# w1's last 96 columns as extra columns of wqkv's third block, with all operations in a fixed order

## The chip, the cores and the metric

The kernel runs on one NeuronCore of a Trainium2 chip. The metric is device time in microseconds; an execution before the change takes 414.9 us (median of three runs, 414.75 to 414.92). One execution was recorded by the hardware profiler. Its page and the answers to queries on its trace are what the sections below quote.

## The reference

Two branches over the normalised input are multiplied and added to the input. Branch A is a causal, dilated sliding-window attention (window 8, step 2, 32 heads of 16), branch B a two-layer MLP on a second LayerNorm of the same rows.

```python
def _A_ref(x, wqkv, wo):                      # S=2048, D=512, H=32, W=8, dil=2
    qkv = (x @ wqkv).reshape(B, S, 3, H, Dh)  # then split and transposed
    ...
    logits = einsum("bhsd,bhswd->bhsw", q, kg) * Dh ** -0.5
    attn = softmax(where(mask, logits, -1e9))
    o = einsum("bhsw,bhswd->bhsd", attn, vg)
    return o.reshape(B, S, D) @ wo

def _B_ref(x, w1, b1, w2, b2):                # w1: 512x1376, w2: 1376x512
    y = _layernorm(x)
    h = gelu(y @ w1 + b1)
    return h @ w2 + b2

xn = _layernorm(x)
return x + _A_ref(xn, wqkv, wo) * silu(_B_ref(xn, w1, b1, w2, b2))
```

## The kernel before

**Tiling.** The 2048 positions fall into two interleaved halves (DIL = 2, since the attention steps by 2) of eight tiles with 128 positions each. Every fp32 operand is held as a high and a low fp16 part. A product is three fp16 matmul series: high by high, low by high and high by low. The normalised, transposed activations are in four buffers yT0 to yT3, one for each *chunk* of 512 positions (chunks 0 and 1 are the first half, 2 and 3 the second).

**Attention units.** There are eight units: two halves times four blocks (hb) of 128 columns of wqkv for each of q, k and v. For a unit, `qkv` (from L720) multiplies, tile by tile, a tile of yT as the stationary operand by 384 columns of weights in 12 matmuls (L746) into a PSUM buffer, and ACT (L763) or, in the first two units, sometimes VectorE (L759) scales it into the buffer U0 or U1, units taking turns. The DMA queue then copies shifted rows inside U (halos). `attention` (from L785) works on VectorE: four products q times k over 2048 columns (L805), each with a sum over the head (L808), a softmax with ACT's exponential (L831), and four products with v (L863; L901 in the last unit). POOL adds the first pair of those four (L873, 2048 columns), VectorE the second (L858), POOL does later folds (L883). The result is split into high and low parts (L846 on ACT, L848 on VectorE) and brought into the transposed buffer oT by a DMA transpose (L851).

**MLP.** w1's 1376 columns are eleven blocks f = 0 to 10, ten of 128 columns and a last one of 96. `mlp1` (L1016) uses a block of w1 as the stationary operand and streams a chunk's 512 positions past it, 12 matmuls for each chunk and block, also for the block of 96. ACT applies bias and GELU (L1033) and makes the high part of h (L1036), VectorE the low part (L1038). `mlp2` (L1052) adds h times w2 into four PSUM banks z0 to z3, one for each tile of the chunk: three matmuls for each bank and block. For the last block h lies in the buffer hlast with a row of ones under it, so that b2 is the 97th row of w2. Behind a chunk's last block ACT applies SiLU, and the gate goes to DRAM (gd). `wo_first` (L929) and `wo_last` (L961) multiply oT by wo and combine it with gate and input (L920, L943; L993, L997, L1000).

**The order.** All operations are entered into a plan with their readers, writers and estimated durations. `Plan.issue` places them one after the other: of the operations that are ready, on all engines, it takes one that can start earliest, a hand-set priority deciding among near ones, and so it fixes each engine's order of instructions. Each engine then runs its own list in that order, held back only by waits on what an instruction reads or overwrites. All DMAs are issued from the SP queue. Weight preparation (sums of squares over each weight for its scale, L421 and L514, then high and low parts, L482, L536, L486, L543) belongs to the first hundred microseconds. Some 24 small matmuls on a constant (L1169) run in the first microseconds of TensorE.

## Time and profile before

| | |
|---|---|
| median of three runs | 414.9 us |
| the profiled execution's own time | 415.18 us |
| its span, from the first to the last instruction | 413.4 us |
| mean granted TensorE clock | 0.999 |
| time between span and the execution's time | 1.8 us |

The page gives in part 1 each engine's busy time, its share of the span and its number of instructions; in part 2 the span in forty slices, one digit for a slice in tenths; in part 4 the chain that ended last. A group's line has its source line, engine, operation, output and input with their shape, the count, and then busy time, mean ns of one, idle time ahead of it and what ended that. A line of the timeline has start, length and work, and in brackets how long the engine was idle before and who ended it. DMA issue lines end in the median time from issue to landing.

### The profile page before, as it was taken

Reading aid. Unit: us, or ns where it says so; the run is one execution under the profiler, and the core shown is the slowest. Engines: PE = TensorE matmul, PEld = TensorE weight load, DVE = VectorE, ACT = ScalarE, POOL = GpSimd, SP = SyncE. Lnnn points to the kernel's source line nnn. Section 1 sums busy time; section 2 is a strip of 40 time slices with the busy share of each in tenths; the row PEclk is TensorE's granted clock in tenths of the full one; section 3 lists DMA queues with packets and bytes.
Section 4 is the critical chain, followed back from the end, with each engine's and each line's share of the span. In section 5 each row is a group of like instructions: output and inputs, shape, how many; then the busy total and the mean of one; then the engine's idle time right before and its main releaser. Section 6 shows DMA issues by size and latency. Waiting matters only on the chain.

```text
span 413.4 us, 5554 instructions
## 1 busy us (share of the span) xinstructions
PE 405.9 (98%) x2083; PEld 206.6 (50%) x2083; DVE 379.5 (92%) x379; ACT 222.1 (54%) x353; POOL 120.3 (29%) x131
## 2 busy tenths in 40 slices
PE   8799999999999999999999999999999999999996
PEld 5555544445654455445544554455455544444443
DVE  4996989998999999989998999999999998999954
ACT  4699899994549655843384252225212393263500
POOL 3834002004380425042504330434033404520021
PEclk9999999999999999999999999999999999999999
DMA  8958717030045137720172034223604244007133
GB/s 281 397 112 258 235 61 230 0 128 1 1 142 152 28 93 183 149 46 2 48 221 75 0 102 116 68 86 88 205 7 122 88 111 145 0 18 238 23 102 131
DMA packets 47211, 46.41 MB, mean 112 GB/s; under 512 B 31785, under 2 KB 32225, under 8 KB 46673
## 3 DMA queue, kind: packets, MB, share of 16 engines
q1 hardware_dynamic: 47184, 46.06, 37.6%
q8 instruction: 16, 0.26, 0.3%
q14 instruction: 11, 0.08, 0.1%
HBM read 24.06 MB, written 7.34 MB: 76 GB/s over the span
## 4 chain that ended last, share of the span: by engine, by line
PE 92%; ACT 3%; issue 1%; DVE 1%; POOL 1%; ACTq 0%
PE z L1052 28%; PE ps L1016 28%; PE ps L746 25%; PE ps L929 5%; PE ps L961 2%; PE z L961 2%; PE pl L746 1%; ACT w L421 1%; PE pl L961 1%; ACT f L673 1%; ACT yT L687 0%; ACT wq L536 0%; POOL wq L471 0%; POOL rb L635 0%; ACT prod L661 0%
## 5 line engine op out<-in xcount | busy, mean ns | idle before, releaser
L1016 PE MATMUL ps<-yT,w 128*128 128x512 f16 (+1 forms) x528 | 120.4, 379 | 0.0
L746 PE MATMUL ps<-wq,yT 128*128 128x384 f16 x708 | 117.0, 326 | 0.2 <-DVE U L759 0.2
L1052 PE MATMUL z<-w,h 128*128 128x512 f16 x480 | 110.4, 379 | 0.0
L746 PEld LDWEIGHTS <-yT 128*128 128x128 f16 x744 | 72.5, 98 | 49.2 <-issue 1.0
L1016 PEld LDWEIGHTS <-w 128*128 128x128 f16 (+1 forms) x528 | 52.8, 100 | 61.0
L805 DVE TENSOR_TENSOR prod<-U 128x2048 f32<-128x2048 f32 x32 | 73.2, 2286 | 2.2 <-POOL prod L883 0.7
L1052 PEld LDWEIGHTS <-h 128*128 128x128 f16 x480 | 46.6, 98 | 55.5 <-issue 0.3
L808 DVE TENSOR_REDUCE L<-prod 128x128 f32<-128x2048 f32 x32 | 73.0, 2281 | 0.4
L1033 ACT ACTIVATE ps<-ps,b1T,hsc 128x512 f32<-128x512 f32 (+1 forms) x44 | 32.9, 748 | 73.4 <-PE ps L1016 72.2
L863 DVE TENSOR_TENSOR prod<-pl,U 128x2048 f32<-128x2048 f32 x28 | 63.2, 2283 | 4.2 <-POOL prod L873 4.1
L763 ACT ACTIVATE U<-ps,cs 128x384 f32<-128x384 f32 x54 | 31.2, 580 | 65.2 <-PE ps L746 65.2
L873 POOL TENSOR_TENSOR prod<-prod,prod 128x2048 f32<-128x2048 f32 x7 | 31.7, 4531 | 113.8 <-DVE prod L863 99.6
L883 POOL TENSOR_TENSOR prod<-prod 128x1024 f32<-128x1024 f32 x14 | 32.9, 2349 | 0.0
L882 POOL COPY gate<-prod 1x1 f32<-1x1 f32 x21 | 5.5, 264 | 91.0 <-DVE prod L805 82.2
L1038 DVE SCALAR_TENSOR_TENSOR h<-ps,hsc,h 128x512 f16<-128x512 f32 x40 | 29.6, 741 | 1.7 <-ACT h L1036 1.4
L1036 ACT ACTIVATE h<-ps,hsc 128x512 f16<-128x512 f32 x40 | 27.3, 684 | 1.3 <-PE z L1052 0.4
L929 PE MATMUL ps<-wo,oT 128*128 128x512 f16 x96 | 21.7, 379 | 0.0
L858 DVE TENSOR_TENSOR prod<-prod,prod 128x2048 f32<-128x2048 f32 x9 | 20.5, 2282 | 0.0
L1033 ACT ACT_TABLE_LOAD x10 | 12.8, 1283 | 8.6 <-PE ps L1016 8.5
L883 POOL TENSOR_TENSOR prod<-prod,prod 128x1024 f32<-128x1024 f32 x7 | 16.4, 2347 | 0.0
L961 PEld LDWEIGHTS <-oT 128*128 128x128 f16 x108 | 10.6, 98 | 10.4
L929 PEld LDWEIGHTS <-oT 128*128 128x128 f16 x96 | 9.4, 98 | 11.2
(179 smaller groups left out, 377.8 us busy)
## 6 DMA issues: line engine op xcount, KB each, us to landing
f<-in_A_x_dram SPq DMA_DIRECT2D x31, 256.0 KB, 3.5
U<-U SPq DMA_DIRECT2D x16, 392.0 KB, 4.0
gd<-f SPq DMA_DIRECT2D x12, 256.0 KB, 3.4
prod<-in_A_x_dram SPq DMA_DIRECT2D x8, 256.0 KB, 6.9
oT<-in_B_w_dram SPq DMA_DIRECT2D x2, 1024.0 KB
yT<-in_B_w_dram SPq DMA_DIRECT2D x2, 1024.0 KB, 7.9
f<-gd SPq DMA_DIRECT2D x8, 256.0 KB, 2.7
out_dram<-f SPq DMA_DIRECT2D x8, 256.0 KB, 2.8
```

The lines of the kernel that those rows point to most:

```text
L746: nc.tensor.matmul(b.t[:, 0:384], y[:, s, k, o:o + P], wq[:, hb, t, k], start=(n == 0), stop=(n == 11))
L763: act(384, lambda i=i, b=b: nc.scalar.activation(U3[:, i:i + 31:15, :], b.t[:, 0:384].rearrange("p (t e) -> p t e", t=3), AF.Identity, sca ...
L805: dve(2048, lambda p2=p2, g=g: nc.vector.tensor_tensor(p2(), q, slots(Ut, KH, 2 * g), op=ALU.mult), qk + [("kh", ub, 0), ("kh", ub, 1), (" ...
L808: dve(2048, lambda pr=pr, g=g: nc.vector.tensor_reduce(L3()[:, 2 * g:2 * g + 2], pr.t.rearrange("p (r f d) -> p r f d", r=2, d=DH), AX.X, ...
L863: dve(2048, lambda: nc.vector.tensor_tensor(pr.t.rearrange("p (r f d) -> p r f d", r=2, d=DH), A3()[:, 2 * g:2 * g + 2].rearrange("p r (f ...
L873: pool(4.75, lambda: nc.gpsimd.tensor_tensor(acc.t, acc.t, p1.t, op=ALU.add), [acc, p1], [acc])
L883: nc.gpsimd.tensor_tensor(x.t[:, 0:1024], x.t[:, 0:1024], y(), op=ALU.add)
L929: nc.tensor.matmul(b.t, oT[:, hb, i // 4, s, i % 4], wo[:, t, hb], start=(hb == 0 and n == 0), stop=(hb == last and n == 2))
L961: nc.tensor.matmul(b.t[:, cols], oT[:, hb, i // 4, s, i % 4], wo[:, t, hb, cols], start=(start and hb == 0 and n == 0), stop=(stop and hb ...
L1016: nc.tensor.matmul(b.t[0:M], w1[:, s, f * 512 + k * M:f * 512 + (k + 1) * M], yT[ch][:, t, k], start=(n == 0), stop=(n == 11))
L1033: act(512, lambda: nc.scalar.activation(b.t[0:M], b.t[0:M], AF.Gelu_apprx_tanh, bias=b1T[0:M, f:f + 1], scale=hsc[0:M, 1:2]), [b, ("b1T",) ...
L1052: nc.tensor.matmul(z.t, hl[s][0:K, t * P:(t + 1) * P], w2[0:K, w, f], start=(f == 0 and n == 0), stop=(f == NF - 1 and n == 2))
```

## The change

Three things change together.

1. w1's last 96 columns move into the weight buffer of wqkv's third block (HLAST = 2), which becomes 480 columns wide. The 12 matmuls for each tile of the two units of that block (unit 2 and unit 6) now give q, k and v and, in columns 384 to 479, the last block's pre-activation with *positions on partitions* and features along the row. ACT takes these 96 columns out (L870 of the changed kernel) into an fp32 buffer for each chunk of the half (hl0 or the tile `first`). For each chunk the new function `last_block` fills the pad and the row of ones (POOL), adds the bias along the row (POOL), applies GELU (ACT), makes the high (ACT) and low part (VectorE), and lets a DMA transpose bring it to features on partitions, back into the same buffer. `mlp1` is no longer called for the last block, and `mlp2` takes its operand from there.
2. The order of all operations is a table of numbers, ORDER, that `issue` follows; the greedy choice is left for when the table is empty.
3. Some estimated durations of the plan, and which tile holds the identity and the constant 1/512, change.

```diff
+HLAST = 2
+ORDER = (
+    0, 1, 2, 19, 126, 110, 131, 118, 127, 108, 109, 122, 130, 120, 123, 237, 20, 21, 124, 111, 125, 22, 23, 117,
...
+)
...
-        order = []
+        order, fixed = [], [self.ops[n] for n in reversed(ORDER)]
         while len(order) < len(self.ops):
             best = None
-            for e, cand in engs.items():
+            if fixed:
+                o = fixed.pop()
+                t = max([self.earliest(o)] + [min(b.ring.free) for b in o.bufs if b.slot is None])
+                assert not o.npred and t < float("inf")
+                best = (t, o)
+            for e, cand in engs.items() if best is None else ():
...
-    wq = sb.tile([P, NHB, 2, KT, 384], F16, name="wq")
-    w1 = sb.tile([P, 2, KT * F], F16, name="w1")
+    wq = [sb.tile([P, 2, KT, 384 + FL * (hb == HLAST)], F16, name=f"wq{hb}") for hb in range(NHB)]
+    w1 = sb.tile([P, 2, W1C[3]], F16, name="w1")
+    wl = wq[HLAST][:, :, :, 384:384 + FL]
...
+    def last_block(ch):
+        n = 4 * FL
+        h16 = R_f.new()
+        v = lambda: h16.t.bitcast(F16).rearrange("p (a t f) -> p a t f", a=2, t=4)
...
+        def pads():
+            nc.gpsimd.memset(v()[:, :, :, FL:P], 0.0)
+            nc.gpsimd.tensor_scalar(v()[:, 0, :, FL], halves[:, 8:12], hsc[:, 2:3], 2.0, op0=ALU.mult, op1=ALU.mult)
+        with prio(PEV):
+            pool(0.9, pads, [("hsc2",), ("hp", j, 0), ("hp", j, 1)], [(h16, 2)], port=False)
+            pool(1.0, lambda: nc.gpsimd.tensor_tensor(x3(), x3(), row, op=ALU.add), xk + [("b1T",)], xk)
+            act(n, lambda: nc.scalar.activation(x, x, AF.Gelu_apprx_tanh), xk, xk,
+                aps=1, table="gelu")
+            act(n, lambda: nc.scalar.activation(v()[:, 0, :, 0:FL], x3(), AF.Identity, scale=hsc[:, 2:3]),
+                xk + [("hsc2",)], [(h16, 0)])
+            dve(n, lambda: nc.vector.scalar_tensor_tensor(v()[:, 1, :, 0:FL], x3(), hsc[:, 2:3], v()[:, 0, :, 0:FL],
+                                                          op0=ALU.mult, op1=ALU.subtract),
+                xk + [(h16, 0)], [(h16, 1)], c=0.125)
+            dst = hlt[ch % 2].rearrange("p a (t x) -> p (a t) x", t=4)
+            dma(P * 2048, lambda: nc.sync.dma_start_transpose(dst, h16.t.bitcast(F16)), [(h16, k) for k in range(3)],
+                [("hl", ch % 2)], rate=140e3, issue=1.3, tail=1.2)
...
-                    nc.tensor.matmul(b.t[:, 0:384], y[:, s, k, o:o + P], wq[:, hb, t, k],
+                    nc.tensor.matmul(b.t[:, 0:wide], y[:, s, k, o:o + P], wq[hb][:, t, k],
                                      start=(n == 0), stop=(n == 11))
...
+            if hb == HLAST:
+                act(FL, lambda i=i, b=b: nc.scalar.activation(
+                    hpt[i // 4][:, (i % 4) * FL:(i % 4 + 1) * FL], b.t[:, 384:384 + FL], AF.Identity, scale=hsc[:, 1:2]),
+                    [b, ("hsc",)], [("hp", i // 4, i % 4)], prio=PEV, after=pl.users([("hp", i // 4, i % 4), ("hl", i // 4)]))
+        for j in range(2 if hb == HLAST else 0):
+            last_block(2 * c + j)
...
     def mlp2(ch, f):
-        hi, lo, K, h, hk = hq.pop(f)
+        if f < NF - 1:
+            hi, lo, K, h, hk = hq.pop(f)
+        else:
+            hi, lo, K = (lambda: hlt[ch % 2][:, 0]), (lambda: hlt[ch % 2][:, 1]), FL + 1
+            h = hk = ("hl", ch % 2)
...
-            if p < len(steps):
+            if p < len(steps) and steps[p][1] < NF - 1:
```

Where the order differs, three places. In the rows below a line number, the operation, output and inputs with their buffer numbers, and the shape; L-numbers of the changed kernel differ from those before.

**ACT, from the start of the kernel.** prod0 and U1 hold wqkv's first and second block as loaded, oT, o160 and h0 parts of w1 as loaded; squares are L514 and L421 before, L588 and L495 now. Before:

```order
L514 ACT_TABLE_LOAD
L514 ACTIVATE wq_78,s1_122<-prod0_93 128x768 x2
L536 ACTIVATE wq_78<-prod0_93,qsc_148 128x384 x4
L514 ACTIVATE wq_78,s3_124<-U1_87 128x768
L687 CAST yT0_82<-z30_146 128x4x128
L514 ACTIVATE wq_78,s3_124<-U1_87 128x768
L659 ACTIVATE rb0_151<-pb0_150,rb0_151 128x1
L661 ACTIVATE prod2_95<-prod2_95,rb0_151 128x512
```

Now:

```order
L588 ACT_TABLE_LOAD
L588 ACTIVATE wq0_77,s1_124<-prod0_95 128x768
L588 ACTIVATE wq1_78,s2_125<-U1_89 128x768
L588 ACTIVATE wq0_77,s1_124<-prod0_95 128x768
L610 ACTIVATE wq0_77<-prod0_95,qsc_150 128x384 x3
L588 ACTIVATE wq1_78,s2_125<-U1_89 128x768
L610 ACTIVATE wq0_77<-prod0_95,qsc_150 128x384
L733 ACTIVATE rb0_153<-pb0_152,rb0_153 128x1
L735 ACTIVATE prod1_96<-prod1_96,rb0_153 128x512
L761 CAST yT0_84<-z30_148 128x4x128
L495 ACTIVATE w1_81,s5_128<-o160_107 128x1024
```

A square over the second block now stands between the two squares over the first, and the first square over w1 comes earlier. 76 matmuls of 384 columns before, and 60 now, stand on TensorE ahead of the matmul that totals w1's squares (L435, now L509).

**VectorE, the end of attention 0.** The four products with v read U0 (L863 before, L972 now). Before:

```order
L863 TENSOR_TENSOR prod2_95<-pl0_142,U0_86 128x2048
L863 TENSOR_TENSOR prod1_94<-pl0_142,U0_86 128x2048
L863 TENSOR_TENSOR prod0_93<-pl0_142,U0_86 128x2048
L1038 SCALAR_TENSOR_TENSOR h1_107<-ps2_141,hsc_154,h1_107 128x512
```

Now:

```order
L972 TENSOR_TENSOR prod2_97<-pl0_144,U0_88 128x2048
L972 TENSOR_TENSOR prod1_96<-pl0_144,U0_88 128x2048
L972 TENSOR_TENSOR prod0_95<-pl0_144,U0_88 128x2048
L1143 SCALAR_TENSOR_TENSOR h2_110<-ps2_143,hsc_156,h2_110 128x512
L617 SCALAR_TENSOR_TENSOR wq2_79<-yT2_86,qsc_150,wq2_79 128x2x384 x2
L972 TENSOR_TENSOR prod1_96<-pl0_144,U0_88 128x2048
```

Two low parts of wqkv's third block now stand ahead of the fourth product. Ahead of that product stand, over all, two low parts of h and one of hlast, two single ones of w2 and two of wqkv fewer than before.

**ACT, the third block's first tiles (unit 2).** Before, the evictions of the unit come behind the GELU and the high part of hlast:

```order
L1036 ACTIVATE hlast_91<-ps1_140,hsc_154 96x512
L701 ACTIVATE mv1_159<-mv1_159 128x1
L703 ACTIVATE f2_98,mv1_159<-f2_98,mv1_159 128x512
L1033 ACTIVATE ps2_141<-ps2_141,b1T_90,hsc_154 128x512
L1036 ACTIVATE h2_108<-ps2_141,hsc_154 128x512
L763 ACTIVATE U0_86<-ps1_140,cs2_115 128x3x128
L482 ACTIVATE wo_81<-yT2_84,osc_158 128x1024
```

Now each tile has two evictions, and other work stands between the tiles:

```order
L870 ACTIVATE hl0_93<-ps2_143,hsc_156 128x96
L866 ACTIVATE U0_88<-ps2_143,cs2_117 128x3x128
L1141 ACTIVATE h1_109<-ps1_142,hsc_156 128x512
L870 ACTIVATE hl0_93<-ps0_141,hsc_156 128x96
L495 ACTIVATE wo_83,s6_129<-yT2_86 128x1024 x2
L866 ACTIVATE U0_88<-ps2_143,cs2_117 128x3x128
L773 ACTIVATE f4_102,mv1_161<-f4_102 128x512
L866 ACTIVATE U0_88<-ps0_141,cs2_117 128x3x128
```

The last block no longer passes through `mlp1` there. On TensorE the order of the matmul groups is finer than before: the three matmuls of one z bank now often stand alone between groups of 12. Ahead of unit 2's first matmul stand 168 matmuls of 384 columns in both orders, and of 512 columns 255 before and 213 now.

72 lines of the change are left out of this document (37 added, 35 removed), and 60 rows, old and new, of the table ORDER.

## The prediction

> **What bounds the kernel now.** I read the page's shares first, then the chain of waits in order of time, then the windows, then the groups kept apart by shape. Page, parts 1 and 2:
>
> ```profile
> span 413.4 us, 5554 instructions
> PE 405.9 (98%) x2083; PEld 206.6 (50%) x2083; DVE 379.5 (92%) x379; ACT 222.1 (54%) x353; POOL 120.3 (29%) x131
> ACT  4699899994549655843384252225212393263500
> PEclk9999999999999999999999999999999999999999
> ```
>
> A busy PE need not be a PE without gaps, so the chain decides (start, length, work), with the windows beside it (stretch, its length, then busy time of PE, PEld, DVE, ACT, POOL):
>
> ```profile
> 31.22 0.16 PE z L435
> 31.39 0.67 PE pl L746 x4
> ...
> 101.60 15.60 PE ps L746 x96
> ...
> 378.65 2.59 PE ps L1016 x12
> ...
> 408.45 1.32 PE ps L961 x12
> ...
> 409.80 0.49 DVE U L993
> ...
> 410.32 0.42 DVE U L1000
> 31.20:409.80 378.60, 378.50 (x1937) 189.91 (x1936) 353.82 (x309) 200.30 (x314) 104.05 (x107) 1.00 0.35 100
> 44.00:393.80 349.80, 335.62 (x277) 1.00 0.33 93
> ```
>
> From 31.2 to 409.8 TensorE has no gap worth a tenth of a microsecond. Three things therefore make the span: the head up to 31.2, in which ACT is the dense engine (digits 9 and 8), the matmul work, and 3.6 us of tail. VectorE is second: between its first attention product and its last head output (44.0 to 393.8, second window, DVE alone) it idles 14.2 of 349.8 us. A change can gain from the matmul work, the head or the tail, and lose by making TensorE wait.
>
> Rates come from the chain, where consecutive starts are real. Twelve 512-column matmuls take 2.59, so 216 ns each; 96 of 384 columns take 15.60, so 162.5 ns. The means in the group table (379 and 326) overlap and are not used.
>
> **The change part by part: TensorE.** w1's last block goes as matmuls of its own and comes back as 96 more columns on matmuls that run anyway.
>
> ```profile
> L1016 PE MATMUL ps<-yT,w 128*96 128x512 f16 x48 | 11.0, 379 | 0.0
> L746 PE MATMUL ps<-wq,yT 128*128 128x384 f16 x708 | 117.0, 326 | 0.2 <-DVE U L759 0.2
> ```
>
> Removed: 48 x 216 ns = 10.4 us. The old block used 96 of 128 output rows but paid for the full stream of 512 tokens. Widened: 16 token tiles x 12 = 192 matmuls. No row has 480 columns; between the two rates a column costs (216 - 162.5)/128 = 0.418 ns, so 96 cost 40 ns and 192 cost 7.7 us. Bounds: 0 if 480 went like 384, 10.3 (192 x 53.5) if like 512. I take 7.7, since the two rates are nearly proportional to columns. Net **-2.7 us**, between -10.4 and -0.1. The Trainium skill (TensorE: Matmul & The Clock Gate, "Wait — 56ns, not 53.3ns?") states N/2.4 GHz plus about 2.5 ns; both rows agree with it, and it would give 202.5 ns at 480 columns and the same -2.7. The second product (w2 with 97 rows) stays at 48 matmuls.
>
> **ACT, DVE, POOL, queue.**
>
> ```profile
> L763 ACT ACTIVATE U<-ps,cs 128x384 f32<-128x384 f32 x54 | 31.2, 580 | 65.2 <-PE ps L746 65.2
> L1036 ACT ACTIVATE h<-ps,hsc 128x512 f16<-128x512 f32 x40 | 27.3, 684 | 1.3 <-PE z L1052 0.4
> L1033 ACT ACTIVATE ps<-ps,b1T,hsc 96x512 f32<-96x512 f32 x4 | 3.0, 743 | 17.2 <-PE ps L1016 17.2
> L1033 ACT ACT_TABLE_LOAD x10 | 12.8, 1283 | 8.6 <-PE ps L1016 8.5
> L1038 DVE SCALAR_TENSOR_TENSOR h<-ps,hsc,h 128x512 f16<-128x512 f32 x40 | 29.6, 741 | 1.7 <-ACT h L1036 1.4
> L486 DVE SCALAR_TENSOR_TENSOR w<-h,hsc,w 128x384 f16<-128x384 f32 x1 | 0.6, 608 | 0.0
> L471 POOL TENSOR_TENSOR wq<-prod,wq 128x384 f16<-128x384 f32 x2 | 1.9, 928 | 0.2
> yT<-f SPq DMA_TRANSPOSE x12, 3.3
> ```
>
> ACT: 16 evictions of 96 columns at about 0.35 (580 less 288 columns at the 0.81 ns between the first two rows) are 5.6; four GELUs and four scalings of 384 columns at about 0.6 are 4.8; three more table loads are 3.8; removed are four GELUs and four scalings, 5.7. About +8.5 on an engine with some 190 us idle. Bounds for a small eviction: 0 and 0.58; even 9 us in all would be covered. DVE: 4 x 0.61 for 4 x 0.74, -0.5. POOL: four bias adds of 384 columns at 0.93 and four fills, bounded by 0 and the same 0.93, against removed fills of hlast; at most +7.5 on 120. Four DMA transposes with 3.3 us from issue to landing. All that late work has to be done before the w2 product of the last block: in the changed order 19 us of matmuls lie between the last widened tile of chunk 0 (tiles 0 to 3) and that product, while eviction, add, GELU, scaling, low part and landing come to 0.35 + 0.93 + 0.6 + 0.6 + 0.6 + 3.3 = 6.4. Hidden; were the cover gone, 6.4 per chunk would show.
>
> **The head.** What counts is when matmuls flow without gaps and how many are done by then. Before: 76 matmuls of 384 columns stand ahead of the total over w1 (L435), which starts at 31.22: as if the stream had begun at 31.2 - 76 x 0.1625 = 18.9. In the changed order 60 stand ahead of it, and ACT reaches it earlier, but its second operation is now a square over wqkv's second block.
>
> ```profile
> 4.49 0.84 ACT L514 ACTIVATE wq<-prod 128x768 bf16<-128x768 f32 x1 [2.48 <-DMA prod<-in_A_wqkv_dram]
> 6.84 0.84 ACT L514 ACTIVATE wq<-prod 128x768 bf16<-128x768 f32 x1 [1.41 <-DMA prod<-in_A_wqkv_dram]
> 8.92 2.13 ACT L536 ACTIVATE wq<-prod,qsc 128x384 f16<-128x384 f32 x4 [1.15 <-DVE qsc L459]
> 9.13 0.33 SPq L1126 DMA_DIRECT2D o<-in_B_w_dram  x1
> SPq L1126 <- DMA U<-in_A_wqkv_dram: 0.6, 1, 0.6
> 22.02 1.90 ACT L421 ACTIVATE w<-oT 128x2048 bf16<-128x2048 f32 x1
> ```
>
> The queue's issue at 9.13 waited for that block, so it lands at about 9.1. The two squares (0.95 each with their accumulator) then end at 11.0, and the first scaling starts after the same 1.15 of totals, near 12.1 instead of 8.92: 3.2 later. Behind it the work up to the last square of w1 is 16.6 us in the changed order (four scalings 2.1, one square 0.9, two scalings of 768 1.8, the w1 squares 5.9, three casts 1.6, two normalisations 2.0, two casts 1.2, two evictions 1.1): 28.7, the total at 28.9. Equivalent start: 28.9 - 60 x 0.1625 = 19.1, so +0.3 with no wait counted. The ACT waits of before in this stretch, 1.4 and 1.15 above among them, show what such a sum leaves open: I take **0**, bounds -1.5 and +1.5.
>
> **The tail.** The last product before is a 256-column piece; now it is three 512-column matmuls into z2, with a 512-column scaling and sum behind.
>
> ```profile
> L993 DVE SCALAR_TENSOR_TENSOR U<-z,osc,U 128x512 f32<-128x512 f32 x3 | 2.3, 750 | 3.0 <-PE z L961 3.0
> L1000 DVE TENSOR_TENSOR U<-U,f 128x512 f32<-128x512 f32 x4 | 3.3, 845 | 0.1
> out_dram<-U SPq DMA_DIRECT2D x7, 256.0 KB, 2.0
> out_dram<-U SPq DMA_DIRECT2D x2, 128.0 KB, 1.7
> ```
>
> 0.75 for 0.49, 0.69 (the sum at 0.845 in the mean, 0.69 where nothing disturbs it) for 0.42, 2.0 for 1.7: **+0.8**, bounds 0 and 1.0.
>
> **The waits that the new order could add.** The decisive place is the third block's first group. Matmul work ahead of it falls from 82.4 to 73.3 us (168 x 0.1625, and 255 or 213 x 0.216), so TensorE is there at 92.5 instead of 101.6. It has three ps banks; its third tile, at 92.5 + 2 x 2.43 = 97.4, needs the first one evicted into U0, and that needs attention 0 to have read U0.
>
> ```profile
> 98.47 2.28 DVE L863 TENSOR_TENSOR prod<-pl,U 128x2048 f32<-128x2048 f32 x1
> L543 DVE SCALAR_TENSOR_TENSOR wq<-yT,qsc,wq 128x768 f16<-128x768 f32 x4 | 3.8, 986 | 0.0
> 136.74 4.55 POOL L873 TENSOR_TENSOR prod<-prod,prod 128x2048 f32<-128x2048 f32 x1 [14.00 <-DVE prod L863]
> 140.32 1.52 DVE L713 TENSOR_TENSOR f<-f,f 128x512 f16<-128x512 f32 x1
> L713 DVE TENSOR_TENSOR f<-f,f x8: 675/680/1520, 140.3 to 177.6; 128x512 f16<-128x512 f32 x8
> ```
>
> Attention 0 now ends with three low parts of h and hlast (2.2), two of w2 (1.5) and two of wqkv (2.0) fewer ahead of it: 100.75 - 5.7 = 95.0. But one low part of wqkv comes 2.9 us behind the product that starts POOL's 4.55 us sum, and reads two SBUF tensors. The last two rows show what happens then: a 0.68 us sum stretched to 1.52, ending at 141.8 just after POOL's end at 141.3. So +1.6: 96.7, eviction 0.58, bank free at 97.3 against a need at 97.4. **0**, with no margin: every microsecond more on DVE costs TensorE one. The bounds are 0 and 14.2 (the idle that DVE now shows between 44.0 and 393.8, come once more on top). At the end DVE has slack:
>
> ```profile
> 392.97 0.75 DVE L848 SCALAR_TENSOR_TENSOR o<-prod,osc,o 128x512 f16<-128x512 f32 x1 [0.79 <-ACT o L846]
> oT<-o SPq DMA_TRANSPOSE x9, 4.4
> ```
>
> That last half of attention 7 ends at 393.7 and lands 4.4 later. In the changed order 5.5 us of matmuls stand from the first that needs it to the end (one tile of 256 columns whole, one of 512 whole, the late thirds of three), so for an end at 409.8 - 2.7 = 407.1 it may come as late as 397.2: 3.5 us of slack.
>
> **Sum.** -2.7 + 0 + 0.8 + 0 = -1.9 on the profiled execution's own time of 415.18 (span 413.4 and 1.8 around it): 413.3. The median of the runs shown is 414.9, 0.3 lower: **413.0 us**.
>
> **Rivals.**
> - **VectorE falls behind (slower).** Place: the pair sums on POOL (4.55 each, seven of them), behind which the new order puts more DVE operations with two SBUF operands; in the second unit a low part of wo follows only 1.3 us into the sum and could wait 3.3. Should the seven units lose 1.2 each on average, 8 us in all, the margins (0.1 here, about 4 at the end) leave TensorE waiting some 4 us: 417. It decides once DVE is 2 us later than the sum above has it. For it: the stretched row, and seven places. Against it: DVE's 14.2 us of idle, part of which can move. The Trainium skill (GPSIMD Engine Reference, "1. Specifications") states that POOL's SBUF interfaces are shared with VectorE, with contention for DVE instructions of two SBUF inputs; by that rule each such place costs, and the stretched row agrees. Chance 0.27.
> - **The head gains.** If ACT's early waits close up, 1.5 comes off the head, and 411.5 results. For it: fewer ACT operations ahead of the w1 total. Against: the late square. Chance 0.18.
> - **No net change.** The wide matmuls cost what 512 columns cost, -0.1, and the tail its 0.8: 415.6. Against it: the proportional rates. Chance 0.15.
> - **The forecast** keeps 0.40.
>
> **How the numbers follow.** A measurement here tells changes of about 0.2% (0.8 us). Faster: forecast and head, 0.58; within 0.2%: 0.15; slower: 0.27. The forecast's own range is 411.8 to 414.0. The range, with a tenth out on each side, takes in the head's gain with a little less stall or cheaper columns below (409.8), and the VectorE case above (418).
>
> **What would show it.** Right: 192 matmuls of 480 columns at 12 in 2.43 us; TensorE without gaps from near 29 to about 407; attention 0 read out near 96.7. Wrong: idle on PE ahead of the widened tiles released by ACT's evictions, DVE operations of 0.7 us stretched beyond 1.5 behind POOL's sums, a stream that starts to flow later than 31, or twelve wide matmuls in 2.59.

## The result, and the profile after

The changed kernel is slower: 429.1 us in the median (four runs, 427.2 to 430.9) against 414.9 for the kernel before (414.75 to 415.6). The ratio is 1.034, with a 95% interval of 1.029 to 1.039. The forecast was 413.0, with 409.8 to 418.0 as the range. The profiled execution is the fastest of the four, 427.23 us, with a span of 425.5 against 413.4; 12.1 us have to be found.

Page, parts 1, 2 and 4, of the changed kernel:

```profile
span 425.5 us, 5482 instructions
PE 404.8 (95%) x2035; PEld 200.6 (47%) x2035; DVE 393.7 (93%) x379; ACT 226.5 (53%) x372; POOL 128.7 (30%) x140
PEclk9999999999999999999999999999999999999996
PE 70%; DVE 16%; issue 5%; DMA 3%; ACT 2%; SPq 1%; DVEq 0%; ACTq 0%
```

VectorE has the same 379 instructions and is busy 14.2 us longer than before (393.7 against 379.5). It now holds 16% of the chain that ended last. The granted clock is whole until the last slice, in which TensorE is done.

The windows of the changed kernel (stretch, its length, then busy time of PE, PEld, DVE, ACT, POOL, the granted clock, the DMA share and GB/s) put TensorE's idle time in its places:

```profile
38.60:138.10 99.50, 94.58 (x464) 44.53 (x461) 94.85 (x100) 76.81 (x145) 32.21 (x32) 1.00 0.33 100
138.10:337.40 199.30, 199.30 (x1010) 98.81 (x1010) 191.66 (x140) 93.15 (x143) 64.75 (x71) 1.00 0.38 93
337.40:380.40 43.00, 41.96 (x209) 20.12 (x206) 42.41 (x27) 17.47 (x24) 12.70 (x13) 1.00 0.34 91
415.90:425.50 9.60, 0.61 (x3) 0.10 (x1) 2.61 (x3) 0.00 (x0) 1.27 (x1) 0.66 0.52 191
```

From 138.1 to 337.4 there is no gap at all. Before it 4.9 us are idle, after it 1.0. The last row begins with the first of the last two evictions and still has 0.6 us of matmuls in it, so from the end of the matmuls to the end of the span it is 9.0 us (9.60 - 0.61), where it was 3.6 before. What those gaps wait for is in the view of waits (engine, line, releaser, us in total, times, longest), of which these are the main rows behind the head:

```profile
PE ps L1125 <- DVE h L1143: 2.3, 2, 1.3
PE ps L1125 <- DVE s L522: 1.7, 1, 1.7
PE ps L1125 <- ACT first L870: 0.9, 1, 0.9
PE ps L1125 <- ACT U L866: 0.8, 1, 0.8
```

Busy ends are modelled, so a wait is sized better from start to start. The next fence shows how: six matmuls start at 135.35 and need 6 x 0.216 = 1.30, so the next was due at 136.65; it started at 138.10, 1.45 late, where the row says 1.29. Counted so, the gaps are 0.95 and 0.39 (at 51.6 and 55.0), 1.89 (110.5), 1.06 (123.7), 1.45 (136.4), 1.14 (362.9) and 0.25 (380): 7.1 us; each is named by the start of the last matmul ahead of it. A further 0.15 lies at 121.3. The kernel before has 0.2 behind its head (at 130.2).

**The stretched operations.** The timeline around one of these waits, that at 136.4 (start, length, engine, line, work, count, idle before) shows POOL's pair sum, VectorE behind it and TensorE behind VectorE:

```profile
132.32 4.52 POOL L982 TENSOR_TENSOR prod<-prod,prod 128x2048 f32<-128x2048 f32 x1 [4.80 <-PE z L1161]
132.87 4.52 DVE L787 TENSOR_TENSOR f<-f,f 128x512 f16<-128x512 f32 x1 [0.69 <-ACT f L786]
137.31 0.74 DVE L1143 SCALAR_TENSOR_TENSOR h<-ps,hsc,h 128x512 f16<-128x512 f32 x1
135.35 1.46 PE L1161 MATMUL z<-w,hl 97*128 97x512 f16 x6
138.10 2.75 PE L1125 MATMUL ps<-yT,w 128*128 128x512 f16 x12 [1.29 <-DVE h L1143]
```

The subtraction, 0.68 us where nothing disturbs it, starts 0.55 into the pair sum and ends 0.5 behind it. The low part of h stands behind it on VectorE, and only that low part frees the bank of ps that TensorE wants next. The largest stretch is beside the last of the seven pair sums:

```profile
346.15 4.82 POOL L982 TENSOR_TENSOR prod<-prod,prod 128x2048 f32<-128x2048 f32 x1 [11.44 <-DVE prod L972]
346.52 5.54 DVE L957 SCALAR_TENSOR_TENSOR o<-prod,osc,o 128x1024 f16<-128x1024 f32 x1
351.98 4.47 DVE L972 TENSOR_TENSOR prod<-pl,U 128x2048 f32<-128x2048 f32 x2
```

1.28 became 5.54, and the products with v behind it need the buffer that it reads. Against the plain time of its group, the operations stretched by over 0.25 us lose: 0.7 (L560 at 40.5), 1.3 and 1.7 (L617 at 90.3 and 102.2), 3.8 (L787), 1.1 (L815 at 182), 4.3 (L957), 0.5 (L1109 in the tail): 13.4 us against 2.6 before.

**The wait at 123.7 has another cause.** ACT's own order stands behind it:

```profile
121.47 1.28 ACT L940 ACT_TABLE_LOAD   x1
122.76 0.63 ACT L940 ACTIVATE L<-L 128x512 f32<-128x512 f32 x1
124.13 0.58 ACT L866 ACTIVATE U<-ps,cs 128x384 f32<-128x384 f32 x1 [0.73 <-PE ps L848]
124.61 0.56 ACT L870 ACTIVATE first<-ps,hsc 128x96 f32<-128x96 f32 x2
```

The eviction at 124.13 and the first of the two at 124.61 are of the unit's last tile, whose matmuls end at 124.1, and it is the bank of that tile that TensorE takes at 124.99. The tile ahead of it was done at 120.86, but its evictions (at 124.83 and 125.25) stand on ACT behind the exponential with its table load and behind those of the last tile. The exponential itself waited for nothing: what it reads was ready at 120.2.

**The tail.** The last matmuls, SP's queue, and the last work of POOL and VectorE:

```profile
413.11 3.40 PE L1070 MATMUL z<-wo,oT 128*128 128x512 f16 x15
413.86 8.63 SPq L1111 DMA_DIRECT2D out_dram<-U  x9
415.90 1.41 DVE L1102 SCALAR_TENSOR_TENSOR U<-z,osc,U 128x512 f32<-128x512 f32 x2 [0.84 <-PE z L1070]
416.73 1.27 POOL L1106 TENSOR_TENSOR U<-U,f 128x512 f32<-128x512 f32 x1 [2.90 <-DVE U L1102]
417.34 1.20 DVE L1109 TENSOR_TENSOR U<-U,f 128x512 f32<-128x512 f32 x1
```

All nine writes of the output are issued only from 413.86 to 422.49. The first waits for POOL's sum that ends at 413.83. The second is the write of the tile whose sum runs on POOL from 416.73 to 418.00. Seven writes stand behind it, six of them with sums that had ended by 415.1.

### The profile page after: what moved, and what is told of

Its sections match the earlier page's. It is cut to its first block, busy times and chain, and to the rows that moved or that the text cites. A ratio compares the mean times of both kernels' runs of the same rounds, so it can differ in the third digit from the quotient of the medians.

```text
span 425.5 us, 5482 instructions
## 1 busy us (share of the span) xinstructions
PE 404.8 (95%) x2035; PEld 200.6 (47%) x2035; DVE 393.7 (93%) x379; ACT 226.5 (53%) x372; POOL 128.7 (30%) x140
## 4 chain that ended last, share of the span: by engine, by line
PE 70%; DVE 16%; issue 5%; DMA 3%; ACT 2%; SPq 1%; DVEq 0%; ACTq 0%
PE ps L848 21%; PE z L1161 20%; PE ps L1125 18%; PE ps L1038 5%; PE ps L1070 2%; DVE prod L972 2%; DVE L L917 2%; PE z L1070 2%; DMA f<-in_B_w_dram 2%; DVE prod L914 2%; DVE wq L617 2%; PE pl L848 1%; DVE h L1143 1%; DMA U<-in_A_wqkv_dram 1%; DVE o L957 1%
## 5 line engine op out<-in xcount | busy, mean ns | idle before, releaser
L848 PE MATMUL ps<-wq,yT 128*128 128x384 f16 (+1 forms) x708 | 130.1, 337 | 1.4 <-ACT yT L761 1.0
L1125 PE MATMUL ps<-yT,w 128*128 128x512 f16 x480 | 109.0, 379 | 5.7 <-DVE h L1143 2.3
L1161 PE MATMUL z<-w,h 128*128 128x512 f16 x480 | 113.0, 379 | 0.1
L1125 PEld LDWEIGHTS <-w 128*128 128x128 f16 x480 | 46.8, 98 | 61.8 <-issue 7.0
L972 DVE TENSOR_TENSOR prod<-pl,U 128x2048 f32<-128x2048 f32 x28 | 63.1, 2283 | 0.4
L982 POOL TENSOR_TENSOR prod<-prod,prod 128x2048 f32<-128x2048 f32 x7 | 34.8, 4970 | 60.7 <-DVE prod L972 55.9
L1138 ACT ACTIVATE ps<-ps,b1T,hsc 128x512 f32<-128x512 f32 x40 | 29.8, 747 | 31.4 <-PE ps L1125 31.3
L991 POOL COPY gate<-prod 1x1 f32<-1x1 f32 x21 | 4.5, 214 | 128.9 <-DVE prod L914 119.2
L1038 PE MATMUL ps<-wo,oT 128*128 128x512 f16 x96 | 21.9, 379 | 0.0
L955 ACT ACTIVATE o<-prod,osc 128x1024 f16<-128x1024 f32 (+1 forms) x9 | 9.5, 1055 | 21.5 <-DVE prod L967 14.9
L957 DVE SCALAR_TENSOR_TENSOR o<-prod,osc,o 128x1024 f16<-128x1024 f32 (+1 forms) x9 | 14.7, 1633 | 0.8 <-ACT o L955 0.8
```

Source lines behind the costliest of these rows:

```text
L848: nc.tensor.matmul(b.t[:, 0:wide], y[:, s, k, o:o + P], wq[hb][:, t, k], start=(n == 0), stop=(n == 11))
L972: dve(2048, lambda: nc.vector.tensor_tensor(pr.t.rearrange("p (r f d) -> p r f d", r=2, d=DH), A3()[:, 2 * g:2 * g + 2].rearrange("p r (f ...
L982: pool(4.75, lambda: nc.gpsimd.tensor_tensor(acc.t, acc.t, p1.t, op=ALU.add), [acc, p1], [acc])
L1038: nc.tensor.matmul(b.t, oT[:, hb, i // 4, s, i % 4], wo[:, t, hb], start=(hb == 0 and n == 0), stop=(hb == last and n == 2))
L1125: nc.tensor.matmul(b.t[0:M], w1[:, s, f * 512 + k * M:f * 512 + (k + 1) * M], yT[ch][:, t, k], start=(n == 0), stop=(n == 11))
L1138: act(512, lambda: nc.scalar.activation(b.t[0:M], b.t[0:M], AF.Gelu_apprx_tanh, bias=b1T[0:M, f:f + 1], scale=hsc[0:M, 1:2]), [b, ("b1T",) ...
```

## The experiments

Line numbers of the experiments differ from the changed kernel's by one to three (in e7 and e8, whose table is empty, by some sixty). Numbers in the diffs are rows of ORDER, each one operation of the plan. Each run's time is its median, the ratio that to the kernel before on the same chip.

| run | what is changed | us | ratio [95%] |
|---|---|---|---|
| | the changed kernel | 429.1 | 1.034 [1.029, 1.039] |
| e1 | order of the output writes | 424.8 | 1.024 [1.021, 1.026] |
| e2 | two swaps on VectorE | 426.0 | 1.026 [1.024, 1.029] |
| e3 | POOL's pair sum in four pieces | 427.7 | 1.031 [1.028, 1.035] |
| e4 | loads of w2 earlier on SP | 426.0 | 1.026 [1.024, 1.028] |
| e5 | e1 + e2 + e4 | 420.6 | 1.013 [1.011, 1.015] |
| e6 | e5 + e3 | 421.6 | 1.015 [1.013, 1.018] |
| e7 | no table, the planner with the new constants | 425.4 | 1.025 [1.023, 1.028] |
| e8 | no table, the planner with the old constants | 415.3 | 1.000 [0.999, 1.002] |
| e9 | pair sums left out | 424.5 | 1.023 [1.021, 1.026] |
| e10 | e8's order, loads of w2 earlier | 414.7 | 0.999 [0.998, 1.000] |
| e11 | as e10, both loads first | 415.0 | 1.000 [0.999, 1.001] |
| e12 | as e10, one first, all the rest behind the halo | 414.9 | 1.000 [0.999, 1.001] |
| e13 | a square in the head later | 428.3 | 1.033 [1.031, 1.035] |
| e14 | e5 + e13 + three more moves | 418.7 | 1.009 [1.008, 1.011] |
| e15 | e10, total over w2 earlier | 416.3 | 1.004 [1.002, 1.005] |
| e16 | e15, a low part of h first | 418.5 | 1.009 [1.006, 1.012] |
| e17 | e14 + the first tiles' normalisation earlier | 418.6 | 1.009 [1.007, 1.010] |

**e1: the queue of writes.** The end of the table:

```diff
-    1245, 1246, 1247, 1218, 1238, 1223, 1228, 1243, 1248, 1233, 1257, 1253,
+    1245, 1246, 1247, 1233, 1223, 1228, 1218, 1243, 1253, 1257, 1238, 1248,
```

> Only the order of the nine writes of the output on SP's queue is changed, to the order in which their sums end in the changed kernel's trace (the two whose sums end at 418.0 and 418.5 go last). Theory A (the tail is a queue blocked by its second write, whose sum on POOL ends at 418.0): the last write is issued right behind the last sum, the time from the end of the matmuls to the end of the span falls from 9.6 to about 5.6, so 4 us less than the changed kernel, near 425. Rival (the writes would anyway be held by the last sum and by their own transfers): less than 1 us, 428 to 430.

424.8 us, 4.4 less. In e1's chain and timeline the last work has the same shape, but only two writes are left for the time behind it:

```profile
span 423.0 us, 5485 instructions
414.40 2.60 PE z L1068 x12
417.02 1.42 DVE U L1100 x2
419.14 0.88 SPq L1109 DMA_DIRECT2D out_dram<-U  x2
```

From the start of the last two evictions to the end of the span it is now 6.0 us (423.0 - 417.0) instead of 9.6. So 3.6 of the 5.4 that the tail had gained was the queue: every write waits on SP for its own sum, and nothing behind it goes out. In the changed kernel's trace the second write is let go at 418.02 and the seven behind it back to back between 418.46 and 422.49. The Trainium skill (DMA: Bandwidth & Descriptors, "Anatomy of one DMA — SWDGE (gpsimd) path") says that the DMA engines wait on no semaphore and that such a wait is served by the issuing sequencer ahead of dispatch; these writes, issued by SP, agree.

**e2: VectorE at two places.**

```diff
-    547, 282, 255, 503, 504,
+    547, 503, 282, 255, 504,
...
-    341, 567, 299,
+    567, 341, 299,
```

> Two swaps on VectorE alone. In the second unit a low part of wqkv and one of w2 go behind the reduction that stood behind them, so they come after POOL's 2.3 us sum and not into it; and a low part of h goes ahead of the subtraction that waited 3.8 us behind POOL's pair sum. Theory A (TensorE's waits at 110.5, 123.7 and 136.4, 4.4 us together, are VectorE held by POOL's sums, with banks of ps queued behind it): those waits go to under 1 us together, 3 to 4.4 us less, about 425.5. Rival (TensorE waits there for something else, or the time is lost again later): 428 to 430.

426.0 us, 3.2 less, inside what the theory gave. The waits of 1.89 and 1.45 are gone. The one of 1.06 stayed (122.9), as ACT's order did, and a new one of 1.33 came at 144.5, also for a low part of h; so part of what VectorE gains is lost again.

**e3: is it the running POOL instruction that VectorE waits for?**

```diff
-            pool(4.75, lambda: nc.gpsimd.tensor_tensor(acc.t, acc.t, p1.t, op=ALU.add), [acc, p1], [acc])
+            def quarters():
+                for q in range(0, 2048, 512):
+                    nc.gpsimd.tensor_tensor(acc.t[:, q:q + 512], acc.t[:, q:q + 512], p1.t[:, q:q + 512], op=ALU.add)
+            pool(4.75, quarters, [acc, p1], [acc])
```

> POOL's pair sum is four sums of 512 columns in place of one of 2048; nothing else. Theory A (a VectorE operation with two SBUF operands waits until the POOL instruction that runs has ended): no VectorE operation is held for more than some 1.5 us, VectorE's busy time falls from 393.7 by 5 to 8, and the waits at 136.4 and 362.9 shrink, 2 to 3 us less than the changed kernel, about 427. Rival (POOL and VectorE share bandwidth and the whole sum counts): the same stretched times, 429.

At the same place the subtraction is over after 1.22 us, while POOL's four pieces are still running:

```profile
133.35 6.39 POOL L982 TENSOR_TENSOR prod<-prod,prod 128x512 f32<-128x512 f32 x4 [4.74 <-DVE prod L970]
133.95 1.22 DVE L785 TENSOR_TENSOR f<-f,f 128x512 f16<-128x512 f32 x1 [0.68 <-ACT f L784]
135.20 0.75 DVE L1144 SCALAR_TENSOR_TENSOR h<-ps,hsc,h 128x512 f16<-128x512 f32 x1
```

No operation beside a pair sum loses more than 1.1 (the largest in the changed kernel was 4.3); the low part behind a fold on POOL, which is not cut, still loses 1.7. VectorE is busy 388.2 instead of 393.7, and the wait at 136.4 is gone. So what VectorE waits for is the end of the POOL instruction that runs, not of the whole sum. POOL pays: four pieces take 4.95 where no such VectorE operation comes between (at 258.1) and 6.39 here, the one sum 4.52. The time fell by 1.5 us, inside the changed kernel's own scatter; the one at 362.9 grew from 1.14 to 1.58.

**e4: the loads of w2.**

```diff
-    306, 105, 160, 103, 161, 101, 162, 307, 303, 404, 102, 104,
+    306, 105, 103, 101, 160, 161, 162, 307, 303, 404, 104, 102,
```

> On SP's queue alone: two 256 KB loads of w2 go ahead of a halo copy, the third ahead of the second 1 MB load. Theory A (the square over w2's last pieces at 51.4 was late by that load, and held ACT and with it the evictions): the waits of TensorE at 51.6 and 55.0, 1.35 us together, vanish, about 427.8. Rival (the halo copies become late in their place and attention 0 starts later): no gain or 1 to 2 us more.

426.0 us, 3.2 less, with no wait of TensorE at 52 or 55. In the changed kernel's chain the last 256 KB piece of w2 is issued behind two halo copies and a 1 MB load and lands 7.7 us later, ACT waits 2.12 for it, and the evictions wait behind that on ACT:

```profile
42.49 0.55 SPq L880
43.09 0.58 SPq L1239
43.73 7.68 DMA f<-in_B_w_dram
52.62 0.61 ACT w L1338 x2
53.24 1.89 ACT w L495 x2
```

The gain is larger than the 1.35 of the profiled execution. That wait differs between executions: in e1, e2, e3, e9 and e13, which do not touch it, the gap near 52 alone is 1.51, 2.14, 0.95, 1.55 and 2.19, in the changed kernel's own trace 0.95. In e13 TensorE also runs at half its clock behind that gap and loses another 1.7 (last section). The changed kernel's four runs spread over 3.7 us, e4's over 0.7 (425.5 to 426.2). That the load makes the scatter is not shown by this: e5 and e6 below have the same loads and spread over 1.8 and 2.1.

**e5 and e6: together.**

> The writes, the two swaps and the w2 loads of the first three edits together. Theory A (three separate losses: a blocked queue in the tail, VectorE held by POOL, a late load): the gains add up, 4.4 + 3.2 + 3.2 = 10.8 less than the changed kernel's 429.1, so 418.3; what then stays above before is a head of about 2, a tail of about 2 and some 3 us of other waits, against 2.7 of matmuls saved. Rival (they hide one another, TensorE waits later in their place): 421 to 424.

> The same three edits, and POOL's pair sum in four pieces. If POOL's hold on VectorE still costs after the swaps (1.3 at 91.5, 1.9 at 134.0, 4.3 at 345.7), it gives 1 to 2 us more than the three edits alone, about 417; if what is left is not on the path, the same as these.

420.6: 8.5 of the 10.8 add up. The waits that stay are 1.06 (119.7), 1.33 (141.2) and 1.13 (358.7). The pieces on top give nothing: 421.6, and the runs of the two overlap (419.5 to 421.3 and 420.7 to 422.7).

**e7 and e8: the columns without the table.** ORDER is empty in both, so the planner orders the operations; e8 has also the three estimates of the kernel before:

```diff
-ORDER = (0, 1, 2, 19, ...)
+ORDER = ()
...
-            self.dma += o.nbytes / (o.rate if self.dma > SLOW else 250e3)
+            self.dma += o.nbytes / (o.rate if self.dma > SLOW else 265e3)
...
-        pool(0.42 + n * 3.05e-3, fn, **k)
+        pool(0.45 + n * 3.9e-3, fn, **k)
...
-            pool(2.1, lambda: nc.gpsimd.tensor_scalar(x(), x(), mv0[:, q, 0:1], rb0[:, q:q + 1], op0=ALU.subtract,
+            pool(1.25, lambda: nc.gpsimd.tensor_scalar(x(), x(), mv0[:, q, 0:1], rb0[:, q:q + 1], op0=ALU.subtract,
```

> The columns moved as in the change, with the change's three cost constants, but the table of numbers is empty, so the planner that orders the kernel before places every operation. Theory A (the loss lies in the order that the table fixes, not in the columns): 412 to 418, near the kernel before, as the matmul work is 2.7 us less. Rival (the moved columns themselves cost, by their evictions, their sums on POOL and the late second half): 425 or more, as with the table.

> As the run before, with the planner's three cost constants of the kernel before: what the column move does by itself. Theory A: 411 to 417, and the tail and the load of w2 as before. Rival: 425 or more.

e8 answers the main question. With the moved columns, ordered by the planner of before, the kernel takes 415.3, as the kernel before does (ratio 1.0003). So all of the loss lies in the order. e7 misses its expectation: three estimates in the planner, none of which changes an instruction, move its result by 10 us. Its waits are near 62 and 64 (2.3 and 2.1) and at 134 (3.9), and behind them TensorE's granted clock is 0.52 (66.9 to 70.2) and 0.54 (138.3 to 142.0), which costs another 3.2. e8's page and waits:

```profile
span 413.7 us, 5501 instructions
PE 403.7 (98%) x2035; PEld 201.1 (49%) x2035; DVE 385.0 (93%) x379; ACT 228.1 (55%) x371; POOL 127.7 (31%) x140
PE z L1099 <- DVE w L498: 1.2, 1, 1.2
PE ps L1063 <- DVE h L1081: 0.9, 2, 0.7
```

TensorE is busy 2.2 us less than before (403.7 against 405.9), and waits 3.0 us in the middle of e8, from start to start (0.83, 1.35, 0.43 and 0.34), where it had waited 0.2: the saving is eaten there.

**e9: what the pair sums cost in all.**

```diff
-            pool(4.75, lambda: nc.gpsimd.tensor_tensor(acc.t, acc.t, p1.t, op=ALU.add), [acc, p1], [acc])
+            pool(4.75, lambda: nc.gpsimd.tensor_tensor(acc.t[:, 0:8], acc.t[:, 0:8], p1.t[:, 0:8], op=ALU.add), [acc, p1], [acc])
```

> The changed kernel with POOL's seven pair sums of attention cut to 8 of 2048 columns each, which leaves that part of the sum over the pairs out. It bounds what these sums cost by holding VectorE. Theory A: the stretched operations at 91, 133, 181 and 346 shrink to their plain times (10 of 13.4 us of stretch go, VectorE's busy time falls to about 384), the waits at 136.4 and 362.9 vanish, the one at 110.5, which lies behind another POOL sum, shrinks with VectorE being 1.3 earlier; 3 to 5 us less than the changed kernel, 424 to 426, while head, load of w2 and tail keep the rest. Rival (POOL's hold is the main cost): 420 or less.

424.5 us, 4.7 less. VectorE's stretches fall from 13.4 to 3.3 us, its busy time to 384.2, the waits at 136.4 and 362.9 are gone, that at 110.5 is 0.55. The 1.06 behind ACT is as it was. The hold of the pair sums on VectorE thus makes about a third of the loss, nearly all of the waits behind VectorE (4.2 of 4.7) and none of the tail.

**e10 to e12, e15 and e16: can the column move gain?** e8's order as a table, the first 1 MB load of w2 ahead of the first halo copies and the second right behind them (e10); both ahead (e11); one ahead, the small pieces and the second behind the copies (e12):

```diff
-    160, 161, 162, 163, 164, 102, 165, 103, 104, 105,
+    102, 160, 161, 162, 163, 164, 105, 165, 103, 104,
```

> The moved columns with the order that the planner of before gives, fixed as a table, and one edit on SP's queue: the first 1 MB load of w2 ahead of the first halo copies, the second right behind them. In the column move by itself the second lands at 56.6, and the total over w2 behind it costs TensorE 0.8 at 59.2 and 1.35 at 62.6. Theory A (that load is what is late): both waits go, 2 us less than the column move by itself, about 413.3, which is below before by 0.4%. Rival (halo copies late, attention 0 later): 415 or more.

> As the run before, but both 1 MB loads of w2 ahead of the first halo copies. Theory A: w2 is there even earlier, but TensorE needs no more than the run before gives: 413 to 413.5. Rival: 2 MB ahead of the halo copies take some 6 us of the queue's transfers, attention 0 starts up to 4 later, and the time is 415 to 418.

> First 1 MB load ahead of the halo copies, then the two small pieces of w2 and the second 1 MB behind them, ahead of the small patch of the halo. Theory A: as the first of these three, 413 to 413.5. Rival: the patch of the halo is late, 414 to 416.

The wait of 0.83 went, that of 1.35 became 1.66 in all three: the load was early, but the total over w2 stands behind 60 matmuls on TensorE. 414.7 (e10) is 0.1% below before, which is no change by the bound of 0.2%. e15 moves that total forward on ACT, TensorE and VectorE (in this order below, the rows of one engine at a time). e16 does so too, but has 426, 246, 434, 248 on ACT and 382, 244, 420, 247, 385, 383 on VectorE:

```diff
-    411, 412, 418, 238, 419, 426, 434, 246, 248,
+    238, 411, 412, 418, 419, 426, 246, 248, 434,
...
-    425, 433, 243, 441,
+    243, 425, 433, 441,
...
-    382, 385, 420, 244, 383, 247,
+    382, 244, 385, 420, 247, 383,
```

> As the first run with w2's 1 MB loads ahead (414.7), and the total over w2 is taken earlier on each engine: its second square on ACT ahead of two GELUs, its matmul ahead of two groups, its small VectorE steps ahead of a product, two scalings of w2 and the first low part ahead of a reduction. Theory A (that total's place is what held TensorE for 1.66 at 61.4): the wait goes, 1.5 less, about 413.2, below before by 0.4%. Rival (evictions of ps become late instead): 414.5 or more.

> As the run with w2's total taken earlier, but the low part of h that freed its bank late (61.0) goes ahead of the attention product on VectorE, and one GELU goes between two scalings of w2 on ACT. Theory A (a second wait hid behind the first, both are order alone): neither the 1.66 at 61.4 nor the 2.35 at 58.5 is there, 414.7 - 1.5 = 413.2, below before by 0.4%. Rival (VectorE, behind by the product that is moved back, makes TensorE wait later): 414.5 to 416.

Both miss. The wait is gone at 61.4 and is there elsewhere, larger each time: 2.35 at 58.5 in e15, 3.83 at 69.2 in e16, and each is for a low part of h on VectorE; behind the last, e16's clock is halved as in e7 (0.52 from 73.2 to 76.6):

```profile
PE z L1159 <- DVE h L1141: 3.7, 1, 3.7
```

**e13, e14 and e17: the head and the rest.** e13 puts one square behind others (166 from ahead of 33 to ahead of 167). e14 adds this to e5, and on ACT 478 and 477 ahead of the exponential 518, on VectorE 583 ahead of 527, and 1092 ahead of 1102. e17 is e14 with steps of the first tiles' normalisation (51, 52, 69, 71, 72) ahead of what they stood behind; the "table of before" in its expectation is e14's.

> The changed kernel with one move on ACT: the square over the later of two blocks of wqkv, which waits until 8.9 for its load, goes behind the square over the first block's second half and the three scalings that need only that. Theory A (the late square held the first block's total, VectorE behind it and so the normalised tiles): the first total is ready near 8.9 and not 11.5, the matmuls flow 1.5 to 2 us earlier, about 427.3. Rival (the head is bound by something later, such as the statistics on VectorE): less than 0.5 us, 428.6 to 429.6.

> The three edits of before (writes, swaps, loads of w2), the head's move, and three moves at the waits that stayed: on ACT two evictions go ahead of an exponential with its table load, on VectorE a low part of h goes ahead of the last pair sum of a unit, and a low part of the attention output goes ahead of the product that starts POOL's pair sum. Theory A (all that is left is order): the waits at 119.7, 141.2 and 358.7, 3.5 us together, go down to about 1, the head gains 1.5, 420.6 - 4 = 416.5. Rival (VectorE and ACT are full there and the waits only move): 419 to 421.

> The reordered table of before (418.7), and in the head the first tile's cast and low part, the third group's small steps behind its statistics and the last tile's normalisation each go ahead of work that the first matmuls do not need (statistics for later, wqkv totals, POOL's low part). Theory A (the head is the order of the first tiles' normalisation): the last of the four tiles is normalised near 18.6 and not 20.3, the matmuls flow 1 to 2 us earlier, 417.0 to 417.7. Rival (the loads or the totals of wqkv bound the head): 418.4 to 419.

e13 misses: the first scaling came at 9.96 instead of 11.55, the stream only 0.3 earlier. That is inside what the head varies by from one execution to the next: with the head as in the changed kernel, its equivalent start (total over w1 less 60 matmuls) is 21.0 there and in e2, 21.9 in e3 and 20.2 in e5. e14 falls between theory and rival: the wait on ACT is gone, that at 358.7 fell to 0.45, that at 141 grew to 1.89 (143.8). e17 misses and shows why. The last of the first four tiles is normalised at 16.8, 3.4 earlier than in the changed kernel (20.3), and TensorE then waits for the other operand, the second block of wqkv:

```profile
15.57 1.28 DVE L740 TENSOR_SCALAR prod<-prod,mv,rb 128x512 f32<-128x512 f32 x2
19.86 0.48 PE L846 MATMUL ps<-wq,yT 128*128 128x384 f16 x2 [1.63 <-ACT wq L608]
20.68 1.62 PE L846 MATMUL ps<-wq,yT 128*128 128x384 f16 x7 [0.34 <-ACT wq L608]
```

Two chains, the tiles and that block's scaling, end almost together; taking one away leaves the other.

## Why the prediction was wrong, point by point

By the prediction's own terms, against the profiled execution:

| term | forecast | measured |
|---|---|---|
| matmul work | -2.7 | -2.7 |
| head (equivalent start of the stream) | 0, within 1.5 | +2.2 |
| waits behind VectorE | 0, within 14.2 | +4.7 |
| waits behind ACT's order | not in the sum | +1.2 |
| a late load of w2 | not in the sum | +1.35 |
| tail | +0.8, up to 1.0 | +5.4 |

The sum is 12.15; less the 0.2 that the kernel before also waits it is 11.95, against 12.1 of span. The median lies another 1.9 above the profiled execution; a longer wait for the load of w2 is likely to be part of that, but the slower executions have no trace. Two steps of the forecast failed by most: it took the waits behind VectorE from one place and put them at 0, and it sized the tail by the length of its last piece and not by SP's queue.

**Right: the matmuls.** Twelve wide ones take 2.43 us (the chain, in a stretch without gaps), as worked out from the two rates:

```profile
275.41 2.43 PE ps L848 x12
L848 PE MATMUL ps<-wq,yT 128*128 128x480 f16 x192 | 40.5, 366 | 0.0
```

That is 202.5 ns each, which the Trainium skill's rule (TensorE: Matmul & The Clock Gate, "Wait — 56ns, not 53.3ns?") gives too. "12 in 2.59" did not come.

**Right: ACT, POOL and the four transposes are covered.** ACT rose by 4.4 (226.5 against 222.1), not 8.5; POOL by 8.4, where the bound was 7.5. The two transposes of the late half whose landing the trace has land in 3.1 us, and no matmul with hl waits for one. Since e8 needs no more time than before, with this work in it, none of it is the cause.

**Right, and misleading: the decisive place.** The third block's first group starts at 95.92, and attention 0's last product ends at 95.79; the forecast had 92.5 and 96.7. With the head 2.2 later and 1.35 lost to w2, 92.5 becomes 96.0. The third tile, which needs attention 0 read out and one eviction of 0.58, starts at 95.92 + 2 x 2.43 = 100.78. TensorE came 3.4 later than forecast and VectorE 0.9 earlier, so the place had 4.4 us in hand, and there is no wait. The 0 came true here, but the margin of 0.1 that it rested on was never put to the test:

```profile
93.52 2.28 DVE L972 TENSOR_TENSOR prod<-pl,U 128x2048 f32<-128x2048 f32 x1
95.92 9.88 PE L848 MATMUL ps<-wq,yT 128*128 128x480 f16 x48
```

The step that failed is to take this one place for all. "Every microsecond more on DVE costs TensorE one" held, 15 us later: the low parts behind POOL's sums at 90.3 and 102.2 had cost VectorE 3.0 us by then, and it freed the next bank of ps at 112.6, 1.89 late. With the 1.3 at 90.3 gone (e9) that wait is 0.55. The next one, 1.06, is ACT's order and stays in every run with that order (e1 to e6, e9, e13); e14, which changes it, is without it; the 1.45 and the 1.14 are again VectorE behind pair sums.

**The rival that came true, in part.** "VectorE falls behind" had the right mechanism and the chance 0.27. Its stretch was low: seven places at 1.2 are 8 us, measured are 13.4, of which 10.5 beside four of the seven pair sums and nothing beside the other three, because two operations started right behind POOL's (0.55 and 0.4 into it) and waited for nearly the whole sum. For "some 4 us" of waits 4.7 came. By itself that would have made 413.0 + 4.7 = 417.7, inside the range; tail, head, ACT's order and the load of w2 brought the rest. With the Trainium skill's row on the shared SBUF interfaces (GPSIMD Engine Reference, "1. Specifications") these rows agree. The price is what e3 shows: the time up to the end of the POOL instruction that runs. That VectorE's idle of 14.2 before should speak against this rival was the wrong weight: such idle is of no use where it does not stand. In the changed kernel 7.6 us of it lie between 138.1 and 337.4, where nothing waits.

**The tail: mis-sized by 4.6.** The sum counted the durations of the last piece and not the queue. The order of SP's writes was in the change, and a product's place in TensorE's order against its write's place on SP would have shown it: the second write's sum is the last but one to end. e1 takes 3.6 of it away. The rest, 1.8, is the longer last piece, with POOL's sum of 1.27 in it and VectorE's last sum stretched from 0.69 to 1.20 beside that.

**The head: the marker was wrong.** The total over w1 stands at 30.79 in the changed kernel, 60 matmuls behind the start, so the stream starts as if at 30.79 - 60 x 0.1625 = 21.0 instead of 18.9:

```profile
30.79 0.17 PE L509 MATMUL z<-s,fours 128*128 128x4 bf16 x1
17.19 0.56 ACT L761 CAST yT<-z 128x512 f16<-128x512 f32 x1
```

The forecast took ACT's work up to that total (28.9) as what binds. TensorE binds there: its first tile is cast at 17.2, where the kernel before casts it at 13.55, and the waits of the matmuls that follow are for tiles (0.97, 0.87 and 0.24, up to 23.3). The late square, which the forecast had seen, is not the reason by itself (e13): the scaling came 1.6 earlier and the stream 0.3. That the second block's scaling ends close behind the tiles is shown (e17), and which orders would bring both forward was not found. With starts from 20.2 to 21.9 for the same order, the 2.2 is known to about a microsecond.

**The load of w2** has no term in the forecast: it followed SP's issues in the head alone, and in the tail it counted only transfers.

**Open.** How far the order can be mended is open. e14 takes 10.4 of the 14.2 us back and leaves waits for VectorE. And the column move by itself gains nothing in any order that was run, though it takes 2.7 us off TensorE: the waits it leaves are mostly on VectorE again, which is at 93% busy in e8 as well. That VectorE is what bounds this kernel next is an inference from e10, e15 and e16, not shown by a run that makes VectorE's work less; e9 comes closest, and it does so in the slower order.

## What to carry to other kernels

Where an engine that works through its list in order is 93% busy next to one at 95 to 98%, a changed order is priced at every place where the one frees a buffer for the other, not at the tightest one: the lateness of one place arrives at the next. Follow each queue of DMAs to its end, the output writes above all: a write whose data come last, placed second, holds all that are behind it. And separate an edit from the order it comes with: the same columns in the order of the planner of before cost nothing, with the table the loss was 14 us.

## What the runs showed of the hardware that was not expected

- A VectorE instruction with two SBUF operands that starts while POOL runs a sum of two SBUF operands, of 384 columns or more, ends only behind it, up to 4.3 us late; of 262 such cases in all the traces together none ended ahead of POOL. It is not so beside POOL's short powers of 8 columns: a low part of wo at 122.14 took its plain 1.28 inside one that ran from 121.72 to 123.69. POOL waits likewise: its pair sum at 220.25, begun 0.26 behind a product of q and k that ran to 222.27, took 6.42 instead of 4.5. Operations with an operand in PSUM went on beside it: of the products with v, two of 2.28 each took 4.48 together, one of them beside the sum:

```profile
84.96 4.48 DVE L972 TENSOR_TENSOR prod<-pl,U 128x2048 f32<-128x2048 f32 x2
87.32 4.53 POOL L982 TENSOR_TENSOR prod<-prod,prod 128x2048 f32<-128x2048 f32 x1 [10.68 <-DVE prod L972]
```

- It holds for each instruction: cut in four, POOL's sum lets VectorE in between (e3).
- Behind some waits TensorE runs at half its clock for about 3 us. In e13, behind the gap of 2.19 near 52, twelve matmuls of 512 columns take 4.22 us instead of 2.75, and from 55.1 on they start 0.427 apart instead of 0.216; the second row is the window with its granted clock:

```profile
53.65 4.22 PE L1123 MATMUL ps<-yT,w 128*128 128x512 f16 x12 [2.03 <-ACT U L864]
53.64:58.30 4.66, 4.65 (x15) 1.85 (x15) 3.18 (x3) 4.66 (x7) 0.00 (x0) 0.63 0.00 1
```

  The same is in e7 (twice) and e16, each time for 1.5 to 1.7 us more. It did not come behind 2.14 in e2 or 2.35 in e15, nor in the changed kernel's profiled execution, whose longest wait behind the head is 1.89. What decides it, no run here shows.
- A load of 256 KB that was issued right behind one of 1 MB landed 7.7 us behind its issue; another of the three, issued ahead of that, took 4.3.
